# Handing out side work by an engine-time allowance, with loads' copies pinned and sums joined

## The chip, the cores and the metric

The kernel runs on one core of a Trainium2 chip. The metric is device time in microseconds (us) for one execution, from the first to the last instruction and a little around it. Five engines work side by side, each through its own instructions strictly in the order in which they stand: PE (TensorE, matrix products), DVE (VectorE), ACT (ScalarE), POOL (GpSimd) and SP (SyncE, which only issues transfers). An instruction that waits holds up everything behind it on its engine.

## The reference

Four batches of 10048 tokens with 128 channels go through an attention over 49 agents, and the result through a mixture of experts (4 groups of 4 experts, the best group and the best expert of it taken per token).

```python
def sm(a, b):
    s = scale * (a @ b.transpose(0, 2, 1))
    s = s - s.max(-1, keepdims=True)
    e = np.exp(s)
    return e / (e.sum(-1, keepdims=True) + 1e-09)
agent_v = sm(agents, k) @ v          # per batch: 49 x 128
x = sm(q, agents) @ agent_v          # per batch: 10048 x 128
...
g_sm = np.exp(g_logits - g_logits.max(-1, keepdims=True))
g_sm /= g_sm.sum(-1, keepdims=True) + 1e-09      # likewise e_sm in the group
h = np.maximum(xg[mask_e] @ w1[g, e], 0.0)
ye = h @ w2[g, e]
out[tok_idx] = (g_w * e_w)[:, None] * ye
```

## The kernel before

**Units.** The main work is a stream of 644 units. A unit takes one tile of 512 tokens and one eighth of an expert's 1024 hidden columns: `first` (L1139) makes two products into a PSUM tile `ph`, lets ACT write the rectified fp16 part `hh`, and lets DVE write the fp16 remainder `hl` (one `SCALAR_TENSOR_TENSOR` out of `ph` and `hh`); `second` (L1155) makes twelve products into `po` from `hh` and `hl`. There are 3 `ph` tiles, so the products of unit k+3 wait for the `hl` of unit k, and `second` runs 8 units behind `first`. Three batches (positions 0 to 2 in `SEQ`) go through one common expert each, 20 tiles of 8 units, 480 units together; the fourth batch is sorted by expert into DRAM (`sorted_rows`) and makes the last 164 units. Before the first unit, one batch's keys and values are worked off alone.

**Side work.** Everything else is written as Python generators ("lanes") that are drawn on between two units while the program is being written out; a `yield` is a place where the writer may go back to the units, and a `yield n` asks for n units of rest. Lanes `k1` to `k3` (`agents`, L481) do the keys and values of a batch: `xh`, the fp16 part of the keys, on ACT, `xl`, the remainder, on POOL, scores on PE, largest values `mch` on DVE, then `vh` on ACT and `vl` on DVE (`value_split`, L439). Lanes `q0` to `q3` do the queries' weights (`query_exp`, L649: `mq` and `ef` on DVE, the exponential on ACT). Lanes `a0` to `a3` (`followed`, L615) do the routing of five parts of a batch: `routing` (L776) and `weigh` (L817) are long rows of small DVE operations on tiles of 20 columns (`rm`, `rc`, `oh`, `rx`, `rd`, `rrg`, `rre`, `cw`) with two exponentials `rd<-rd` on ACT. `expert_load` and `expert_split` (L1073, L1083) fetch an expert's weights (`w1f`, `w2f`) and split them into fp16 parts. `p3` sends the rows of the sorted batch to DRAM; only when all lanes have ended does `ahead` fetch the first sorted tiles (`er`) and weights (`wbuf<-wdr`).

**What sets the order.** `advance` (L1317) goes through the lanes after each unit. `QUEUE` gives each lane a start and an end in batches; a lane is drawn on for as long as its share of the counted cost `TOTALS` is behind that line, however many steps that takes, and an `a` lane gets up to three steps a unit. `own_tile` and `run_second` draw on a lane by force where a tile needs what isn't there yet. Afterwards a scheduler places each instruction in its engine's order, and may put one ahead of where it was written if it takes its inputs to be there early enough; `keep_in_program_order` pins an instruction behind all that was written for its engine before it.

Of the kernel before, what the change touches and what calls it, by code (L numbers as in the profile page):

```python
# [13 lines left out]
AF = mybir.ActivationFunctionType  # L14
ALU = mybir.AluOpType
# [8 lines left out]
C = 128  # L24
# [4 lines left out]
FB = F // P  # L29
# [21 lines left out]
W2S = 256.0  # L51
# [4 lines left out]
HT = CT // 2  # L56
VS = 16.0
# [8 lines left out]
SORTS = ((0, 5), (5, 10), (10, 15), (15, OT))  # L66
ST = 5 * TQ
ORDER = "kkkkkmkvkvqkqmvvqvvvv"
POOLED = "01001001"
KA = 2  # L70
QUEUE = (("a0", 0.0, 9.0), ("a1", 0.0, 9.0), ("a2", 0.0, 9.0), ("a3", 0.0, 9.0),
# [63 lines left out]
def build(ctx, tc, qT, kT, v, agT, wr, w1, w2, cpk, out):  # L135
    nc = tc.nc
    pool, sync = nc.gpsimd, nc.sync
    work = np.zeros(3)
    pe = Counted(nc.tensor, work, 0, 4.0, 0.42)
    vec = Counted(nc.vector, work, 1, 65.0, 1.04)  # L140
    act = Counted(nc.scalar, work, 2, 190.0, 0.83)
# [127 lines left out]
    clock, forced = [0], [False]  # L269
# [169 lines left out]
    def value_split(b, ci):  # L439

        st = state[b]
        vf = st.pop(("v", ci))
        sh, sl = [mo.tile([P, CT, NA], F16, name=name) for name in ("sh", "sl")]
        vh, vl = [wk.tile([P, CT * P], F16, name=name, tag="x" + name[1]).rearrange("p (t c) -> p t c", c=C) for name in ("vh", "vl")]
        parts = value_parts(b, ci)
        for x, y, m in parts:
            act.activation(vh[0:m, y], vf[0:m, y, 0:C], AF.Copy, scale=VS)
        yield 1
        for x, y, m in parts:
            act.activation(sh[0:m, y], x, AF.Copy)  # L450
            vec.scalar_tensor_tensor(out=vl[0:m, y], in0=vf[0:m, y, 0:C], scalar=VS, in1=vh[0:m, y], op0=ALU.mult, op1=ALU.subtract)
        yield 1
        for x, y, m in parts:
            for a in range(0, x.shape[1], HT):
                z = slice(a, min(x.shape[1], a + HT))
                pool.tensor_sub(out=sl[0:m, y][:, z], in0=x[:, z], in1=sh[0:m, y][:, z])  # L456
        yield
        st["v", ci] = sh, sl, vh, vl
# [190 lines left out]
    def query_exp(b, ci, x, early):  # L649
        t0, t1 = chunks[ci]  # L650
        nt = t1 - t0
        psv = x["ps"][:, 0:nt * NA].rearrange("p (t a) -> p t a", a=NA)
        mq = sm.tile([P, CT], F32, name="mq")
        vec.tensor_reduce(out=mq[:, 0:nt], in_=psv, axis=AX.X, op=ALU.max, negate=True)
        x["ef"] = ef = wk.tile([P, CT, NA], F32, name="ef")
        vec.tensor_add(out=ef[:, 0:nt], in0=psv, in1=mq[:, 0:nt].unsqueeze(2).broadcast_to([P, nt, NA]))
        yield HOP
        act.activation(ef[:, 0:nt], ef[:, 0:nt], AF.Exp)
        yield
# [116 lines left out]
    def routing(b, t0, t1):  # L776

        st = state[b]
        r0 = t0 // ST * ST
        r = t0 // ST  # L780
        lg = st["lg", r]
        if t0 == r0:
            st["ohf", r] = pc.tile([P, NG + NE, ST], F16, name="oh")
            st["g", r] = [pc.tile([P, ST], F32, name=name) for name in ("gm", "zz", "zr")]
        o = st["ohf", r]
        gm, zz, zr = st["g", r]
        flat = lambda a: a.rearrange("p s i t -> p (s i) t")
        t = slice(t0 - r0, t1 - r0)
        pair = lg[:, 0:NG + NE, t].rearrange("p (k j) t -> p k j t", j=2)
        op = o[:, :, t].rearrange("p (k j) t -> p k j t", j=2)  # L790
        mt = sm.tile([P, (NG + NE) // 4, 2, ST], F32, name="rm")[:, :, :, 0:t1 - t0]
        ct = sm.tile([P, (NG + NE) // 4, 2, ST], F16, name="rc")[:, :, :, 0:t1 - t0]
        vec.tensor_tensor(out=op[:, :, 1], in0=pair[:, :, 0], in1=pair[:, :, 1], op=ALU.is_ge)
        vec.tensor_tensor(out=flat(mt), in0=pair[:, :, 0], in1=pair[:, :, 1], op=ALU.max)
        yield
        vec.tensor_tensor(out=ct[:, :, 0], in0=mt[:, :, 0], in1=mt[:, :, 1], op=ALU.is_ge)
        vec.tensor_tensor(out=ct[:, :, 1], in0=mt[:, :, 0], in1=mt[:, :, 1], op=ALU.is_lt)
        vec.tensor_max(out=gm[:, t], in0=mt[:, 0, 0], in1=mt[:, 0, 1])
        vec.tensor_mul(out=op[:, :, 0], in0=op[:, :, 1], in1=flat(ct))
        vec.tensor_sub(out=op[:, :, 1], in0=flat(ct), in1=op[:, :, 0])  # L800
        yield
        og = o[:, 0:NG, t].unsqueeze(2).broadcast_to([P, NG, 4, t1 - t0])
        oh = o[:, NG:, t].rearrange("p (g e) t -> p g e t", g=NG)
        vec.tensor_mul(out=oh, in0=oh, in1=og)
        if t1 == NTP:
            vec.memset(o[:, NG:, NT - r0:], 0.0)
            vec.memset(o[LAST:P, NG:, NT - 1 - r0:NT - r0], 0.0)
        st["oh"] = o[:, NG:, t]
        if t1 % ST == 0:
            sync.dma_start(out=ohd[b][:, r], in_=o[:, NG:])  # L810
        yield
        vec.tensor_scalar(out=zz[:, t], in0=lg[:, NG + NE, t], scalar1=1e-9, scalar2=None, op0=ALU.add)
        vec.reciprocal(out=zr[:, t], in_=zz[:, t])
        vec.tensor_scalar(out=zr[:, t], in0=zr[:, t], scalar1=st["scb"][:, 1:2], scalar2=None, op0=ALU.mult)
        yield

    def weigh(b, t0, t1):  # L817

        st = state[b]
        r = t0 // ST  # L820
        n, t = t1 - t0, slice(t0 - r * ST, t1 - r * ST)
        lg, ohf, g = st["lg", r], st["ohf", r], st["g", r]
        og = ohf[:, 0:NG, t]
        gm, zz, zr = [a[:, t] for a in g]
# [8 lines left out]
        def numerators(x, largest):  # L833
            bc = lambda a: a.unsqueeze(1).broadcast_to([P, 4, n])
            d = sm.tile([P, 4, ST], F32, name="rd")[:, :, 0:n]
            vec.tensor_sub(out=d, in0=x, in1=bc(largest))
            vec.tensor_mul(out=d, in0=d, in1=bc(zr))
            yield HOP
            act.activation(d, d, AF.Exp)
            yield HOP  # L840
            return d

        x = sm.tile([P, NG, 4, ST], F32, name="rx")[:, :, :, 0:n]
# [6 lines left out]
        sg = yield from numerators(lg[:, 0:NG, t], gm)  # L850
        sg = fold(sg, ALU.add, "g")
        yield
        se = yield from numerators(el, fold(el, ALU.max, "m"))
        se = fold(se, ALU.add, "e")
        yield
        for y in (se, sg):
            vec.tensor_scalar(out=y, in0=y, scalar1=1e-9, scalar2=None, op0=ALU.add)
        vec.tensor_mul(out=sg, in0=sg, in1=se)
        vec.tensor_mul(out=sg, in0=sg, in1=zz)
        yield  # L860
        vec.reciprocal(out=sg, in_=sg)
        if t0 == 0:
# [220 lines left out]
    def expert_split(b, x, ws):  # L1083

        w1f, w2f = x["w"]
        for h in range(2):
            ps = bank()
            s = slice(h * 512, (h + 1) * 512)
            pe.matmul(ps, state[b]["at"], w1f[:, s], start=True, stop=True)
            yield HOP  # L1090
            act.activation(ws[:, s], ps, AF.Copy)
            vec.tensor_sub(out=ws[:, F + h * 512:F + (h + 1) * 512], in0=ps, in1=ws[:, s])
            yield
        wv = ws[:, 2 * F:].rearrange("p (k h c) -> p k h c", k=FB, h=2)
        act.activation(wv[:, :, 0], w2f, AF.Copy, scale=W2S)
        yield
        vec.scalar_tensor_tensor(out=wv[:, :, 1], in0=w2f, scalar=W2S, in1=wv[:, :, 0], op0=ALU.mult, op1=ALU.subtract)
        yield

    def kept_expert(b, x, j):  # L1100

# [203 lines left out]
    def step(lane):  # L1305
        if not lane["live"]:
            return 0
        w = work.copy()
        y = next(lane["gen"], "end")
        if y == "end":  # L1310
            lane["live"] = False
        lane["done"] += (y if y in (0, 1) else 0) if lane["name"][0] == "p" else float(np.dot(work - w, WL))
        if lane["name"][0] != "p":
            lane["until"] = clock[0] + (y if isinstance(y, int) else 0)
        return y

    def advance(part):  # L1317
        clock[0] += 1
        for lane in lanes:
            if not lane["live"] or part <= lane["start"]:  # L1320
                continue
            kind = lane["name"][0]
            if kind == "k" and any(y["live"] for y in lanes[:lanes.index(lane)] if y["name"][0] == "k"):
                continue
            if kind == "p":
                if clock[0] % 3:
                    step(lane)
                continue
            if lane["until"] > clock[0]:
                continue  # L1330
            steps = 0
            while lane["live"] and (kind == "a" and steps < 3 or kind != "a" and (part >= lane["end"] or lane["done"] < lane["total"] * (part - lane["start"]) / (lane["end"] - lane["start"]))):
                steps += 1
                if isinstance(step(lane), int):
                    break

    def lane(name):
        return next(y for y in lanes if y["name"] == name)
# [26 lines left out]
    live, fetched, loads = {}, 0, 0  # L1365
# [13 lines left out]
    for pos, i in stream:  # L1379
        if pos < NOWN:  # L1380
            x = own_tile(pos, i)
# [3 lines left out]
        else:  # L1385
# [7 lines left out]
            x = live.pop(i)  # L1393
# [45 lines left out]
```

## Time and profile before

| | us |
|---|---|
| median of 3 runs (1019.42 to 1022.51) | 1021.24 |
| the profiled execution, its own time | 1021.64 |
| its span in the profile | 1019.8 |
| span before the first unit's `hh` | 77.8 |
| units with side work, 78 to 757 us | 679 |
| last own units, almost without side work, 757 to 817 us | 60 |
| sorted units | 187 |

The profile is of one execution. Busy shares over the span are means over these stages: in the last two PE has no idle time, and in the one from 78 to 757 us four engines share the work. The granted clock is PE's, as a share of 2.4 GHz; its other level is 0.5, that is 1.2 GHz.

### The profile page before, as it was taken

The page shows a single profiled execution, that of the slowest core. Times are in us where ns is not written, and L with a number is a line of the kernel's source. Part 1 is how long each engine was busy: PE and PEld are TensorE (multiplying, and loading weights), DVE is VectorE, ACT ScalarE, POOL GpSimd, SP SyncE. Part 2 cuts the span into 40 slices and gives each one's busy share as a digit, 9 for nine tenths or more (in the row PEclk, how much of TensorE's full clock was granted, in tenths as well). Part 3 has the DMA queues.
Part 4 walks back from the last instruction along what each step waited for, and adds up shares of the span by engine and source line. Part 5 has one row for each costly group of instructions (what it writes and reads, how often), then busy time and mean ns, then how long its engine had stood idle before and what let it go on. Part 6 is the DMA issues. An engine that isn't in the chain of part 4 may idle for free.

```text
span 1019.8 us, 31244 instructions
## 1 busy us (share of the span) xinstructions
PE 910.4 (89%) x12947; PEld 725.0 (71%) x12948; DVE 788.2 (77%) x1785; ACT 633.4 (62%) x1086; POOL 430.8 (42%) x569
## 2 busy tenths in 40 slices
PE   3848898899889999899888989899899999999994
PEld 2835677787667778777676777687677877777884
DVE  5636899878879687897897989899786666666663
ACT  4517687676668666867666766665555565555552
POOL 3108643441833354823452244655455114444444
PEclk9778899999999999989999999999999999999998
DMA  9636543332572443724315131213643535544551
GB/s 310 195 107 198 165 126 108 118 96 93 162 223 77 133 125 95 217 85 134 107 46 175 41 113 30 90 57 113 210 166 105 176 129 185 175 162 164 176 192 37
DMA packets 107511, 138.14 MB, mean 135 GB/s; under 512 B 7479, under 2 KB 88186, under 8 KB 104160
## 3 DMA queue, kind: packets, MB, share of 16 engines
q1 hardware_dynamic: 102208, 125.75, 38.9%
q0 software_dynamic: 5152, 10.30, 3.1%
q8 instruction: 103, 1.69, 0.7%
q14 instruction: 48, 0.39, 0.1%
HBM read 96.83 MB, written 39.45 MB: 134 GB/s over the span
## 4 chain that ended last, share of the span: by engine, by line
PE 51%; DVE 23%; issue 7%; ACT 7%; POOL 6%; DMA 5%; SPq 1%; POOLq 0%; ACTq 0%; DVEq 0%
PE po L130 25%; PE ph L130 17%; PE at L130 8%; DVE hl L130 8%; POOL xl L266 4%; DVE vl L130 2%; DMA w2f<-w 2%; ACT hh L130 1%; DMA vf<-v 1%; DVE oh L130 1%; DMA erow<-rows 1%; ACT xh L130 1%; DVE oo L130 1%; DMA out<-oo,er 1%; DVE rrg L130 1%
## 5 line engine op out<-in xcount | busy, mean ns | idle before, releaser
L130 DVE SCALAR_TENSOR_TENSOR hl<-ph,hh 128x512 f16<-128x512 f32 (+1 forms) x644 | 432.4, 680 | 138.9 <-ACT hh L130 137.6
L130 PEld LDWEIGHTS <-hh 128*128 128x128 f16 x5104 | 422.6, 99 | 148.8 <-issue 8.9
L130 PE MATMUL po<-wbuf,hh 128*128 128x128 f16 x5104 | 507.5, 221 | 0.0
L130 ACT ACTIVATE hh<-ph 128x512 f16<-128x512 f32 (+1 forms) x644 | 376.4, 592 | 195.4 <-PE ph L130 194.5
L130 PE MATMUL po<-wbuf,hl 128*128 128x128 f16 x2552 | 468.1, 221 | 0.0
L130 PE MATMUL ph<-et,wbuf 98*128 98x512 f16 (+2 forms) x1312 | 390.3, 380 | 33.4 <-DVE hl L130 31.4
L266 POOL TENSOR_TENSOR xl<-xf,xh 128x256 f16<-128x256 f32 x280 | 188.4, 709 | 200.0 <-ACT xh L130 176.3
L130 PEld LDWEIGHTS <-hl 128*128 128x128 f16 x2552 | 251.5, 99 | 1.5 <-issue 0.3
L130 PEld LDWEIGHTS <-wbuf 98*128 98x128 f16 (+1 forms) x1412 | 108.6, 100 | 59.7 <-issue 41.2
L1192 POOL DMA_INDIRECT out<-oo,er x82 | 80.6, 984 | 137.7 <-ACT hh L130 92.3
L971 POOL DMA_INDIRECT sorted_rows<-rows,slot x79 | 79.7, 1009 | 78.1 <-ACT hh L130 58.7
L456 POOL TENSOR_TENSOR sl<-S,sh 128x245 f16<-128x245 f32 (+2 forms) x51 | 35.3, 716 | 116.2 <-ACT sh L130 104.0
L130 ACT ACTIVATE xh<-xf 128x1280 f16<-128x1280 f32 (+2 forms) x59 | 73.6, 1252 | 16.4 <-PE at L130 10.3
L130 PE MATMUL at<-agh,xl 128*128 128x49 f16 x553 | 56.4, 186 | 9.0 <-POOL xl L266 8.8
L130 PEld LDWEIGHTS <-xh 128*128 128x128 f16 (+1 forms) x1164 | 55.3, 98 | 6.8 <-issue 3.7
L130 PE MATMUL at<-agh,xh 128*128 128x49 f16 x553 | 56.5, 186 | 2.7 <-ACT xh L130 1.3
L130 PEld LDWEIGHTS <-xl 128*128 128x128 f16 x582 | 48.0, 97 | 13.4 <-POOL xl L266 12.9
L130 PE MATMUL at<-agl,xh 128*128 128x49 f16 x553 | 56.0, 185 | 0.0
L130 ACT ACTIVATE et<-at 98x512 f16<-98x512 f16 (+2 forms) x81 | 46.8, 583 | 12.9 <-PE at L130 9.5
L686 POOL TENSOR_TENSOR rows<-ef,rows 128x245 f16<-128x245 f32 (+1 forms) x62 | 38.6, 645 | 36.3 <-ACT rows L130 36.3
L130 DVE SCALAR_TENSOR_TENSOR vl<-vf,vh 128x1280 f16<-128x1280 f32 (+2 forms) x27 | 38.4, 1429 | 5.3 <-ACT vh L130 5.1
L130 DVE TENSOR_TENSOR oo<-po,cw 128x512 f32<-128x512 f32 (+1 forms) x60 | 40.4, 673 | 0.0
(257 smaller groups left out, 948.5 us busy)
## 6 DMA issues: line engine op xcount, KB each, us to landing
wbuf<-wdr SPq DMA_DIRECT2D x22, 1024.0 KB, 4.8
vf<-v SPq DMA_DIRECT2D x28, 640.0 KB, 6.1
xf<-qT SPq DMA_DIRECT2D x28, 640.0 KB, 4.5
xf<-kT SPq DMA_DIRECT2D x23, 640.0 KB, 4.3
out<-oo SPq DMA_DIRECT2D x57, 256.0 KB, 2.7
erow<-rows SPq DMA_DIRECT2D x13, 510.0 KB, 2.8
er<-sorted_rows SPq DMA_DIRECT2D x19, 256.0 KB, 4.8
wbuf<-kT SPq DMA_DIRECT2D x5, 640.0 KB, 6.8
```

Of the source, the lines that this page charges most:

```text
L130: return f(*a, **k)
L266: pool.tensor_sub(out=xl[:, a:z], in0=xf[:, a:z], in1=xh[:, a:z])
L456: pool.tensor_sub(out=sl[0:m, y][:, z], in0=x[:, z], in1=sh[0:m, y][:, z])
L686: pool.tensor_sub(out=x0[:, a:z, NA:2 * NA], in0=ef[:, a:z], in1=x0[:, a:z, 0:NA])
L971: ins = pool.indirect_dma_start(out=sorted_rows[:, :], out_offset=bass.IndirectOffsetOnAxis(ap=at, axis=0), in_=x, in_offset=None, bounds_ ...
L1192: ins = pool.indirect_dma_start(out=out, out_offset=bass.IndirectOffsetOnAxis(ap=to, axis=0), in_=y, in_offset=None, bounds_check=B * N - ...
```

## The change

`advance` now gives all lanes together an allowance per unit, 900 ns of counted DVE time and 1100 ns of counted ACT time (`RATE`). The lane that is furthest behind its line goes first, one step at a time (an `a` lane counts as a whole batch behind, and gets two steps a unit), until either allowance is used up or no lane is behind. An overdraft is taken off the next units; what is left over is not kept. The counted cost is 65 ns and 1.04 ns a column for DVE, 190 ns and 0.83 ns a column for ACT. `QUEUE` and `TOTALS` are unchanged.

Three more edits go with it. The ACT copies that read a fresh load (`vh<-vf` and the `w2f` copy) are pinned in program order. Long pieces are split: `vl` and the remainder of `w2` are made in two halves with a `yield` between, and `query_exp` yields between its two DVE operations. Small sums are joined: the factor on `zr` goes into the exponential's scale, and two additions and two products on `se` and `sg` become two `SCALAR_TENSOR_TENSOR`.

```diff
+RATE = np.array([900.0, 1100.0])
...
         for x, y, m in parts:
-            act.activation(vh[0:m, y], vf[0:m, y, 0:C], AF.Copy, scale=VS)
+            tc.keep_in_program_order(act.activation(vh[0:m, y], vf[0:m, y, 0:C], AF.Copy, scale=VS))
...
-            vec.scalar_tensor_tensor(out=vl[0:m, y], in0=vf[0:m, y, 0:C], scalar=VS, in1=vh[0:m, y], op0=ALU.mult, op1=ALU.subtract)
+        yield
+        for x, y, m in parts:
+            for a in range(0, x.shape[1], HT):
+                z = slice(a, min(x.shape[1], a + HT))
+                vec.scalar_tensor_tensor(out=vl[0:m, y][:, z], in0=vf[0:m, y, 0:C][:, z], scalar=VS, in1=vh[0:m, y][:, z], op0=ALU.mult, op1=ALU.subtract)
+                yield
...
-        vec.tensor_scalar(out=zr[:, t], in0=zr[:, t], scalar1=st["scb"][:, 1:2], scalar2=None, op0=ALU.mult)
...
-            act.activation(d, d, AF.Exp)
+            act.activation(d, d, AF.Exp, scale=st["scb"][:, 1:2])
...
-        for y in (se, sg):
-            vec.tensor_scalar(out=y, in0=y, scalar1=1e-9, scalar2=None, op0=ALU.add)
-        vec.tensor_mul(out=sg, in0=sg, in1=se)
-        vec.tensor_mul(out=sg, in0=sg, in1=zz)
+        vec.scalar_tensor_tensor(out=se, in0=se, scalar=1e-9, in1=zz, op0=ALU.add, op1=ALU.mult)
+        vec.scalar_tensor_tensor(out=sg, in0=sg, scalar=1e-9, in1=se, op0=ALU.add, op1=ALU.mult)
...
-        act.activation(wv[:, :, 0], w2f, AF.Copy, scale=W2S)
+        tc.keep_in_program_order(act.activation(wv[:, :, 0], w2f, AF.Copy, scale=W2S))
...
+    def behind(lane, part):
+        if lane["name"][0] == "a" or part >= lane["end"]:
+            return 1.0
+        span = lane["end"] - lane["start"]
+        return min(1.0, (part - lane["start"]) / span) * span - lane["done"] / lane["total"] * span
+
     def advance(part):
...
-            while lane["live"] and (kind == "a" and steps < 3 or kind != "a" and (part >= lane["end"] or lane["done"] < lane["total"] * (part - lane["start"]) / (lane["end"] - lane["start"]))):
-                steps += 1
-                if isinstance(step(lane), int):
-                    break
+        while min(tokens) > 0:
+            some = [(-behind(y, part), i) for i, y in enumerate(lanes)
+                    if y["live"] and i not in over and part > y["start"] and y["until"] <= clock[0] and behind(y, part) > 0]
+            if not some:
+                break
+            i = min(some)[1]
+            w = work.copy()
+            y = step(lanes[i])
+            steps[i] += 1
+            if isinstance(y, int) or lanes[i]["name"][0] == "a" and steps[i] == 2:
+                over.add(i)
+            tokens[:] -= (work - w)[1:]
```

On ACT, late in the own units, this is how the copies of the last experts' `w2f` (into `ws` and `wbuf`) and of their `w1` products (`ws<-at`) stand before the change, each `hh` row being that many units:

```order
L130 ACTIVATE hh<-ph 128x512 x7
L130 ACTIVATE et<-at 98x512
L130 ACTIVATE hh<-ph 128x512 x7
L130 ACTIVATE ws<-w2f 128x8x128
L130 ACTIVATE hh<-ph 128x512
L130 ACTIVATE et<-at 98x384
L130 ACTIVATE hh<-ph 128x512 x2
L130 ACTIVATE wbuf_119<-w2f 128x8x128
L130 ACTIVATE hh<-ph 128x512
L130 ACTIVATE lg<-at 128x19x21
L130 ACTIVATE hh<-ph 128x512 x2
L130 ACTIVATE wbuf_120<-w2f 128x8x128
```

And the same place with the change:

```order
L131 ACTIVATE rd<-rd,scb_7589 128x80
L131 ACTIVATE hh<-ph 128x512 x13
L131 ACTIVATE ws<-at 128x512
L131 ACTIVATE hh<-ph 128x512 x2
L131 ACTIVATE ws<-at 128x512
L131 ACTIVATE hh<-ph 128x512
L131 ACTIVATE ws<-w2f 128x8x128
L131 ACTIVATE hh<-ph 128x512 x5
L131 ACTIVATE wbuf_119<-at 128x512
```

The first `w2f` copy stood behind the 408th own unit's `hh` and ahead of the products of its own expert; it now stands behind both of them, at the 438th.

On DVE, near the 110th unit, where the first part of the second batch is routed while its successor's keys are worked off, this is what stands between two `hl` before:

```order
L130 SCALAR_TENSOR_TENSOR hl<-ph,hh 128x512
L130 TENSOR_TENSOR oh<-oh,rc 128x10x8
L130 TENSOR_SCALAR zr<-zr,scb_4384 128x8
L130 TENSOR_TENSOR oh<-rc,oh 128x10x8
L130 TENSOR_TENSOR rd<-lg,gm 128x4x8
L130 TENSOR_TENSOR oh<-oh 128x16x8
L130 TENSOR_TENSOR rx<-lg,oh 128x16x8
L130 TENSOR_REDUCE cnt_4815<-oh 128x16
L130 TENSOR_TENSOR rx<-rx 128x8x8
L130 TENSOR_TENSOR rd<-rd,zr 128x4x8
L130 TENSOR_TENSOR rel<-rx 128x4x8
L130 TENSOR_TENSOR rhm<-rel 128x2x8
```

With the change the same routing stands like this:

```order
L131 SCALAR_TENSOR_TENSOR hl<-ph,hh 128x512
L131 TENSOR_TENSOR needf_4727<-at,less 1x16
L131 TENSOR_TENSOR oh<-oh,rc 128x10x8
L131 CAST need_4729<-needf_4727 1x16
L131 TENSOR_TENSOR rd<-lg,gm 128x4x8
L131 TENSOR_TENSOR oh<-rc,oh 128x10x8
L131 TENSOR_TENSOR rd<-rd,zr 128x4x8
L131 TENSOR_TENSOR oh<-oh 128x16x8
L131 TENSOR_TENSOR rx<-lg,oh 128x16x8
L131 TENSOR_REDUCE cnt_4921<-oh 128x16
L131 SCALAR_TENSOR_TENSOR hl<-ph,hh 128x512
L131 TENSOR_TENSOR rx<-rx 128x8x8
```

Before, fourteen small operations follow the `hl` (the last three are cut here); now nine do, and the `zr` product is gone.

## Rows read from the trace of the kernel before

**Rows 1.** The page: busy us (share of the span) and instructions of an engine.

```profile
PE 910.4 (89%) x12947; PEld 725.0 (71%) x12948; DVE 788.2 (77%) x1785; ACT 633.4 (62%) x1086; POOL 430.8 (42%) x569
```

**Rows 2.** The stretch 78 to 757 us: its us, busy us of PE, PEld, DVE, ACT, POOL, granted clock, DMA.

```profile
78.00:757.00 679.00, 617.53 (x9264) 490.92 (x9265) 582.98 (x1393) 464.27 (x802) 315.09 (x446) 0.96 0.40 121
```

**Rows 3.** Waits from 78 to 817 us: total us, times, longest.

```profile
ACT rd L130 <- DVE rd L130: 42.2, 27, 3.4
PE ph L130 <- DVE hl L130: 31.4, 25, 3.9
...
PE at L130 <- POOL xl L266: 8.8, 27, 0.9
...
ACT ws L130 <- DMA w2f<-w: 5.0, 1, 5.0
ACT vh L130 <- DMA vf<-v: 4.5, 2, 2.4
...
ACT wbuf L130 <- DMA w2f<-w: 3.7, 3, 3.3
```

**Rows 4.** ACT's timeline: the first copy of the last experts.

```profile
730.00 1.06 ACT L130 ACTIVATE ws<-w2f 128x1024 f16<-128x1024 f32 x1 [4.98 <-DMA w2f<-w]
```

**Rows 5.** PE's timeline around the first of these waits, and at the other.

```profile
727.05 0.28 PE L130 MATMUL po<-wbuf,hh 128*128 128x128 f16 x2
...
732.96 0.70 PE L130 MATMUL ph<-et,wbuf 98*128 98x512 f16 x2 [3.39 <-DVE hl L130]
733.46 0.42 PE L130 MATMUL po<-wbuf,hh 128*128 128x128 f16 x2
```

**Rows 6.** ACT's and PE's timelines near 545 us, with the second batch's `w2f` copy.

```profile
543.85 1.06 ACT L130 ACTIVATE wbuf<-w2f 128x1024 f16<-128x1024 f32 x1 [3.27 <-DMA w2f<-w]
...
546.82 0.59 PE L130 MATMUL ph<-et,wbuf 98*128 98x512 f16 x2 [2.55 <-DVE hl L130]
```

**Rows 7.** DVE groups, 78 to 817 us: busy us, mean ns, idle before.

```profile
L130 DVE TENSOR_SCALAR zr<-zr,scb 128x20 f32<-128x20 f32 (+2 forms) x18 | 5.9, 327 | 0.0
...
L130 DVE TENSOR_TENSOR rrg<-rrg,rre 128x20 f32<-128x20 f32 (+2 forms) x18 | 5.0, 278 | 0.3
...
L130 DVE TENSOR_TENSOR rrg<-rrg,zz 128x20 f32<-128x20 f32 (+2 forms) x18 | 4.7, 261 | 0.4
...
L130 DVE TENSOR_SCALAR rrg<-rrg 128x20 f32<-128x20 f32 (+2 forms) x18 | 4.4, 244 | 0.0
...
L130 DVE TENSOR_SCALAR rre<-rre 128x20 f32<-128x20 f32 (+2 forms) x18 | 4.1, 226 | 0.2
...
L130 DVE SCALAR_TENSOR_TENSOR avT<-at,za 128x49 f32<-128x49 f32 x3 | 0.6, 207 | 0.1
```

**Rows 8.** Instructions on tiles `vl` and `rrg`: ns min/median/max, first and last start.

```profile
L130 DVE SCALAR_TENSOR_TENSOR vl<-vf,vh x27: 274/1481/2223, 136.2 to 519.6; 128x1280 f16<-128x1280 f32 x21, 128x1024 f16<-128x1024 f32 x3, 64x128 f16<-64x128 f32 x3
...
L130 DVE TENSOR_SCALAR rrg<-rrg x19: 159/168/647, 65.7 to 745.9; 128x20 f32<-128x20 f32 x13, 128x8 f32<-128x8 f32 x3, 128x12 f32<-128x12 f32 x3
```

**Rows 9.** Timelines near 430 us: POOL, DVE and PE.

```profile
423.50 7.25 POOL L266 TENSOR_TENSOR xl<-xf,xh 128x256 f16<-128x256 f32 x12
...
427.01 3.96 DVE L130 TENSOR_TENSOR oh<-lg 128x200 f16<-128x200 f32 x1
...
433.88 1.01 PE L130 MATMUL ph<-et,wbuf 98*128 98x512 f16 x2 [3.94 <-DVE hl L130]
```

**Rows 10.** ACT's timeline just before the first unit.

```profile
72.54 1.06 ACT L130 ACTIVATE wbuf<-w2f 128x1024 f16<-128x1024 f32 x1 [6.19 <-DMA w2f<-w]
...
76.10 1.27 ACT L130 ACTIVATE xh<-xf 128x1280 f16<-128x1280 f32 x1 [2.02 <-DMA xf<-kT]
```

**Rows 11.** Timelines of SP and PE where the sorted units begin.

```profile
797.23 2.97 SPq L1127 DMA_DIRECT2D er<-sorted_rows  x4
801.04 1.19 SPq L1116 DMA_DIRECT2D wbuf<-wdr  x2
...
817.01 1.02 PE L130 MATMUL ph<-et,wbuf 98*128 98x512 f16 x4
```

More of the change, by code (lines that the diff above doesn't have):

```diff
@@ L654, in query_exp @@
         vec.tensor_reduce(out=mq[:, 0:nt], in_=psv, axis=AX.X, op=ALU.max, negate=True)
+        yield
         x["ef"] = ef = wk.tile([P, CT, NA], F32, name="ef")
@@ L1094, in expert_split @@
         wv = ws[:, 2 * F:].rearrange("p (k h c) -> p k h c", k=FB, h=2)
-        act.activation(wv[:, :, 0], w2f, AF.Copy, scale=W2S)
+        tc.keep_in_program_order(act.activation(wv[:, :, 0], w2f, AF.Copy, scale=W2S))
         yield
-        vec.scalar_tensor_tensor(out=wv[:, :, 1], in0=w2f, scalar=W2S, in1=wv[:, :, 0], op0=ALU.mult, op1=ALU.subtract)
-        yield
+        for h in range(2):
+            z = slice(h * FB // 2, (h + 1) * FB // 2)
+            vec.scalar_tensor_tensor(out=wv[:, z, 1], in0=w2f[:, z], scalar=W2S, in1=wv[:, z, 0], op0=ALU.mult, op1=ALU.subtract)
+            yield
     def kept_expert(b, x, j):
@@ L1315, in step @@
         return y
+    tokens = np.zeros(2)
+    def behind(lane, part):
[3 more added lines that the diff above has]
+        return min(1.0, (part - lane["start"]) / span) * span - lane["done"] / lane["total"] * span
     def advance(part):
         clock[0] += 1
[L1319 to L1331, printed above, removed]
-            while lane["live"] and (kind == "a" and steps < 3 or kind != "a" and (part >= lane["end"] or lane["done"] < lane["total"] * (part - lane["start"]) / (lane["end"] - lane["start"]))):
-                steps += 1
-                if isinstance(step(lane), int):
-                    break
+        np.minimum(tokens + RATE, RATE, out=tokens)
+        over = set()
+        steps = dict.fromkeys(range(len(lanes)), 0)
+        for i, y in enumerate(lanes):
+            if y["name"][0] == "k" and any(z["live"] for z in lanes[:i] if z["name"][0] == "k"):
+                over.add(i)
+            if y["name"][0] == "p":
+                over.add(i)
+                if y["live"] and part > y["start"] and clock[0] % 3:
+                    step(y)
+        while min(tokens) > 0:
[8 more added lines that the diff above has]
+            if isinstance(y, int) or lanes[i]["name"][0] == "a" and steps[i] == 2:
+                over.add(i)
+            tokens[:] -= (work - w)[1:]
     def lane(name):
```

## The prediction

> **What bounds the kernel now.** I read the page first for the shares, then the stretches, then the waits, and only then the timeline at the longest ones. PE is busy for 89% of the span and DVE for 77% [rows 1]. These means hide that the change touches one stretch only: 78 to 757 us, the 430 or so units with side work between them. There PE is idle for 679 - 617.5 = 61.5 us while DVE works for 583.0 of 679 us (86%), ACT for 464.3 (68%) and POOL for 315.1 (46%) [rows 2]. The reader should see that no engine is full, and that the two that are closest to it take turns in being late. The granted clock is 0.96 there [rows 2]; with levels of 1.0 and 0.5, the shortage of 0.04 is 54 us at the lower level, and 27 us of work at full clock that did not get done.
>
> The waits say who PE waits for: `ph` for an `hl` of DVE in 31.4 us, 25 times, up to 3.9 us, and scores for POOL's `xl` in 8.8 us [rows 3]. A `ph` that waits for `hl` is a queue gone dry: three `ph` tiles let PE run about three units ahead, so DVE, or ACT in front of it, must have been late by that much. The timelines at three of the longest show two kinds of lateness. At 730 us ACT stands 4.98 us before a copy of `w2f` that hasn't landed [rows 4], every `hh` behind it waits too, and PE loses 3.39 us [rows 5]; at 543.85 the same with 3.27 us on ACT and 2.55 us on PE [rows 6]. At 427 us it is DVE alone: one `oh<-lg` of 200 columns takes 3.96 us while POOL works through twelve pieces of `xl`, more small operations stand behind it ahead of the next `hl`, and PE loses 3.94 us [rows 9]. After a loss of this size PE also runs slow for a while: a pair of `po` products takes 0.42 us behind the stall of 733 us against 0.28 us ahead of it [rows 5].
>
> **The change part by part.**
>
> *Pinned copies.* With the change the `w2f` copy stands behind its expert's two `w1` products, and for the last experts it moves by thirty units, from 408 to 438. The transfer has landed by then. That takes away PE's 3.39 and 2.55 us [rows 5, 6]. The `vh` copies waited 4.5 us in two places [rows 3], of which I count 1 us on PE, since a wait of 2.4 us or less is about what three `ph` tiles cover. A: -7 us. Bounds: 0, if the wait moves with the copy, and -10.4 us, if all of the `vh` wait counts.
>
> At the start the same pin costs something. The copy of the first batch's `w2f`, at 72.54 us, lies in time in which ACT would wait for a key load anyway, until 76.10 [rows 10]. Pinned, it comes after that load's copy and ahead of the first `hh`: D: +1 us, the copy's own 1.06 us; 0 if the earlier `w1` copy gives the time back.
>
> *Joined sums.* For each of 18 parts of a batch in this stretch DVE loses `zr` times the factor (327 ns), two additions (244 and 226) and two products (278 and 261) [rows 7], 1336 ns. It gains two `SCALAR_TENSOR_TENSOR` of the same size, which the trace doesn't have. The nearest rows are one of 49 columns at 207 ns, and the product of the same operands at 278 [rows 7]. I take 260, since the shape and the operands are the product's: 1336 - 520 = 816 ns, times 18 is 14.7 us of DVE (14.0 to 16.6 by the two rows). The factor now goes into the exponential on ACT, which has a third of its time free.
>
> *Halves.* Splitting `vl` gives 24 more instructions and the `w2` remainders 5. What an extra start costs is read from the smallest and the middle `vl`: 274 ns for 128 columns and 1481 for 1280 [rows 8], so 1.05 ns a column and 140 ns for the start. 29 x 0.14 = 4.1 us. Below, it costs nothing where DVE would have waited. Net, DVE loses 10.6 us of 583. Not all of it reaches the end: DVE is the late one only at the waits. These sums do stand in just the crowded places, so I count somewhat under half. B: -4 us, from 0 to -12.5.
>
> *The allowance.* The longest row of small operations between two `hl` near unit 110 goes from fourteen to nine, about a third off; the key chunks of the second batch, which came in units 110 to 123, now come in 114 to 135. The lateness that can be had back this way is what DVE and POOL still cost PE after A: 31.4 - 5.9 + 8.8 = 34 us [rows 3, 5, 6]. I take a quarter. A third would match the shorter row, but POOL's pace is untouched and the allowance is loose: it counts 65 ns and 1.04 ns a column, 86 ns for an operation of 20 columns that takes 226 to 327 ns [rows 7]. Ten of them fit into a unit, some 2.5 us. C: -8 us. With fewer long stalls less time at the lower clock follows: a quarter of the 27 us above is 7, and half of that is on time that PE sets, so -3 us. Bounds of both: 0, and -34 - 14 = -48.
>
> *What lies behind.* The side work ends later: the expert splits run to unit 455, past 435, and `p3` ends behind unit 467 instead of 460, so the first fetch of sorted tiles and weights comes some 7 units of 1.1 us later, 8 us. It started at 797.23 and its weights were issued at 801.04, for products at 817.01 [rows 11]. 16 us of cover become 8 us, and the cover is gone if the weights need more than that. I count 0, at most +3 us.
>
> Sum against the profiled execution's own time of 1021.64, which is 0.4 us over the median: 1021.6 - 7 + 1 - 4 - 8 - 3 = 1000.6, so **1001 us**.
>
> **A rule weighed against the rows.** One `oh<-lg` took 3.96 us with POOL at work beside it [rows 9], and an addition on 20 columns that takes 159 ns at best and 168 in the middle took 647 [rows 8]. The Trainium skill, GPSIMD Engine Reference, section Specifications, says that GpSimd's SBUF interfaces are shared with VectorE, with contention for VectorE instructions that have two SBUF inputs or a two-port mode. The trace agrees at 427 us, with 3.96 us. By that rule joining sums helps less than the count, since the joined ones have two SBUF inputs as well, and small operations that are spread over more units meet POOL more often.
>
> **The rivals.**
>
> *Only the loads and the sums.* The allowance is too loose to matter, since its prices are a third of the measured ones, and the bursts stay. For it: the price per operation above. Against it: the row of nine where fourteen stood. A and D whole and half of B: 1021.6 - 7 + 1 - 2 = about 1013.5 us.
>
> *POOL takes it back.* There are some 25 small operations in each of 18 parts, 450 in all. A collision costs up to 0.65 - 0.17 = 0.48 us [rows 8], and POOL is at work for 46% of the time [rows 2]. The mean `rrg` addition of 244 ns against 168 [rows 7, 8] says that now one in six collides. If it became one in three, DVE would get 450 x 0.16 x 0.48 = 35 us more; a third of that on the path is 12 us. The sum is then 1021.6 - 7 + 1 - 4 - 11 + 12 = 1012.6 us with C whole and 1023.6 without it. Since collisions make just the bursts that C is to shorten, I put this case at 1018 to 1023 us. The rule above is about this one.
>
> *The exponentials hold ACT.* ACT stood 42.2 us, 27 times, before `rd<-rd` for DVE's product [rows 3], with the next `hh` behind it. The new order still leaves about one unit between the product and its exponential, and spreading a chain over more units puts more `hl` ahead of the product. If each of the 36 exponentials waited the longest of 3.4 us [rows 3], the sum would be 122 us, 80 more. A wait beyond 2.4 us comes through to PE by about 1 us each, 36 us; half of them would do: 1021.6 - 7 + 1 - 4 + 18 = about 1029.6 us, slower. It decides from about 12 more such waits on. Against it: the allowance takes work from ahead of these products as well.
>
> **How the numbers follow.** The forecast has a chance of 0.58, loads and sums only 0.20, POOL 0.12, the exponentials 0.10. The range is 988 to 1020 us: below it lies the forecast with half of C's bound (0.05), above it the exponentials and half of the POOL case (0.16 together). The forecast's own range is 988 to 1012. About 0.3% is what a measurement of this kernel can tell from no change, 1018.2 to 1024.3 us. Forecast and first rival give 0.58 + 0.17 faster and 0.03 the same; POOL 0.02, 0.08 and 0.02; the exponentials 0.01 the same and 0.09 slower: faster 0.77, same 0.12, slower 0.11.
>
> **What would show it.** A: no wait of ACT on a `w2f` transfer past 78 us. B: no `zr<-zr,scb`, the joined ones near 260 ns, DVE's busy time in the stretch 572 us or so. C: `ph` waiting for `hl` for 20 us or less, no single wait over 3 us, and a granted clock of 0.97 or more. D: the first `hh` at about 79 us. It is wrong if `ACT rd` waits 60 us or more, if small operations get slower on average, or if PE stands idle ahead of the first sorted unit.

## The result, and the profile after

The changed kernel takes 1005.59 us (median of four executions, 1003.51 to 1008.70) against 1021.11 us for the kernel before: a ratio of 0.9851, with a 95% interval of 0.9821 to 0.9881. It is faster by 15.5 us; 1001 us was forecast, with a range of 988 to 1020. Ratios, here and below, are taken over the executions within 1.5% of the fastest of the same kernel. The execution shown took 1003.51 us. Its page, with each engine's busy time, answers to [rows 1]:

```profile
PE 900.1 (90%) x12947; PEld 718.8 (72%) x12948; DVE 784.7 (78%) x1758; ACT 636.3 (64%) x1086; POOL 426.2 (43%) x569
```

The same stretch as in [rows 2], in the same columns:

```profile
78.00:757.00 679.00, 624.51 (x9491) 498.17 (x9492) 590.94 (x1388) 475.38 (x818) 315.90 (x450) 0.98 0.40 122
```

In these 679 us PE now gets through 9491 matmuls instead of 9264. It is idle for 54.5 us instead of 61.5, and the granted clock is 0.98 instead of 0.96. DVE is busier than before here since more units fall into the stretch; over the whole page it has lost 3.5 us, where 10.6 were forecast. Over the whole page PE is idle for 101.7 us of its span of 1001.8 (109.4 of 1019.8 before) and is busy for 10.3 us less than in [rows 1], for the same 12947 matmuls: in these two profiles more than half of the gain is in faster matmuls (the ends of matmuls are modelled in a profile).

The waits from 78 to 817 us answer to [rows 3]:

```profile
ACT rd L131 <- DVE rd L131: 33.6, 28, 2.7
...
PE ph L131 <- DVE hl L131: 25.1, 28, 2.1
...
PE at L131 <- POOL xl L267: 8.3, 22, 0.9
...
ACT xh L131 <- DMA xf<-kT: 5.1, 3, 3.6
...
PE at L131 <- ACT xh L131: 3.4, 1, 3.4
```

No row says that ACT waits for `w2f` or `vf`: those 13 us are gone. PE waits 6.3 us less for `hl`, and the longest such wait is 2.1 us where it was 3.9. The last two rows show a wait that has grown: ACT waited 1.6 us for a key load before, once, and PE had no such wait behind it. The timeline of SP, ACT and PE shows where it comes from:

```profile
271.32 0.35 SPq L1082 DMA_DIRECT2D w1f<-w  x1
271.87 0.41 SPq L1083 DMA_DIRECT2D w2f<-w  x1
272.46 1.52 SPq L237 DMA_DIRECT2D xf<-kT  x2
...
279.24 1.27 ACT L131 ACTIVATE xh<-xf 128x1280 f16<-128x1280 f32 x1 [3.63 <-DMA xf<-kT]
...
280.57 0.22 PE L131 MATMUL at<-agh,xh 128*128 128x49 f16 x1 [3.44 <-ACT xh L131]
```

SP issues the next expert's weight loads and then, behind them, the key load that ACT needs first. That load took 6.7 us to land, against 4.3 in the median of this kernel's key loads of that size. So 3.4 us of what was gained elsewhere are given back here; no run changes the order of the loads, so that the weight loads are the cause is likely, not shown.

DVE's groups of the joined sums and of the remainders, as in [rows 7]: busy us, mean ns, idle before.

```profile
L131 DVE SCALAR_TENSOR_TENSOR vl<-vf,vh 128x640 f16<-128x640 f32 (+2 forms) x51 | 43.0, 849 | 5.5 <-ACT vh L131 5.5
...
L131 DVE TENSOR_TENSOR S<-S,mb 128x490 f32<-128x490 f32 (+2 forms) x27 | 19.8, 751 | 0.1
...
L131 DVE SCALAR_TENSOR_TENSOR rre<-rre,zz 128x20 f32<-128x20 f32 (+2 forms) x18 | 4.8, 268 | 0.4
...
L131 DVE SCALAR_TENSOR_TENSOR rrg<-rrg,rre 128x20 f32<-128x20 f32 (+2 forms) x18 | 4.8, 268 | 0.2
```

The joined sums take 268 ns where 260 was assumed.

### The profile page after: what moved, and what is told of

Read it like the earlier page. It is cut to its first block, busy times and chain, and to the rows that moved or that the text cites. A ratio compares the mean times of both kernels' runs of the same rounds, so it can differ in the third digit from the quotient of the medians.

```text
span 1001.8 us, 31196 instructions
## 1 busy us (share of the span) xinstructions
PE 900.1 (90%) x12947; PEld 718.8 (72%) x12948; DVE 784.7 (78%) x1758; ACT 636.3 (64%) x1086; POOL 426.2 (43%) x569
## 4 chain that ended last, share of the span: by engine, by line
PE 51%; DVE 27%; DMA 6%; POOL 5%; ACT 5%; issue 5%; SPq 1%; POOLq 0%; DVEq 0%; ACTq 0%
PE po L131 25%; PE ph L131 17%; DVE hl L131 10%; PE at L131 8%; POOL xl L267 4%; DVE vl L131 2%; DMA xf<-kT 2%; ACT hh L131 2%; DVE oh L131 1%; DVE oo L131 1%; DMA erow<-rows 1%; DVE rd L131 1%; DVE mq L131 1%; DVE ef L131 1%; DVE rx L131 1%
## 5 line engine op out<-in xcount | busy, mean ns | idle before, releaser
L131 PE MATMUL po<-wbuf,hh 128*128 128x128 f16 x5104 | 501.7, 220 | 0.0
L131 PE MATMUL ph<-et,wbuf 98*128 98x512 f16 (+2 forms) x1312 | 386.3, 377 | 26.9 <-DVE hl L131 25.1
L267 POOL TENSOR_TENSOR xl<-xf,xh 128x256 f16<-128x256 f32 x280 | 183.8, 691 | 211.1 <-ACT xh L131 168.1
L131 ACT ACTIVATE xh<-xf 128x1280 f16<-128x1280 f32 (+2 forms) x59 | 73.6, 1253 | 20.5 <-PE at L131 10.6
L693 POOL TENSOR_TENSOR rows<-ef,rows 128x245 f16<-128x245 f32 (+1 forms) x62 | 40.7, 678 | 70.5 <-ACT rows L131 69.2
L131 PEld LDWEIGHTS <-xl 128*128 128x128 f16 (+1 forms) x582 | 48.9, 98 | 12.3 <-POOL xl L267 12.0
L131 DVE SCALAR_TENSOR_TENSOR vl<-vf,vh 128x640 f16<-128x640 f32 (+2 forms) x51 | 43.0, 849 | 5.5 <-ACT vh L131 5.5
```

The source lines that it names most:

```text
L131: return f(*a, **k)
L267: pool.tensor_sub(out=xl[:, a:z], in0=xf[:, a:z], in1=xh[:, a:z])
L693: pool.tensor_sub(out=x0[:, a:z, NA:2 * NA], in0=ef[:, a:z], in1=x0[:, a:z, 0:NA])
```

## The experiments

The first theory was the prediction's own: the pins give 7 us, the allowance about 11 with what the clock follows, the sums 4. The rival was the first of the prediction: the allowance is too loose to do anything. Kernels were timed in three groups, on three chips, each against the kernel before on that chip (medians 1028.0, 1027.6 and 1019.4 us), so ratios are compared rather than times. The kernel before has one profile, which was taken ahead of these groups.

A ratio says nothing of the way in which time was saved. Every timed execution also lists its span and its mean granted clock, so I split the gain in two. (1 - clock) x span is the time that the lowered clock would cost if PE set the pace throughout; for the kernel before in the first group it is 0.0432 x 1026.1 = 44.3 us. What is left of the span is the second part. Both are averaged over the executions of a kernel and subtracted from those of before. The mean clock differs by 0.0035 from one execution to the next, so each part is uncertain by some 3 to 4 us. It is a rough estimate, since the clock's mean also runs over time in which PE does not set the pace. Ahead of the first unit this is plain to see. The stretch from 20 to 60 us, first in the profile above and then in that of the same kernel's last run below:

```profile
20.00:60.00 40.00, 30.73 (x323) 27.27 (x323) 20.48 (x46) 15.37 (x26) 8.27 (x10) 1.00 0.59 177
```

```profile
20.00:60.00 40.00, 30.29 (x323) 26.86 (x323) 20.63 (x47) 15.23 (x25) 8.27 (x10) 0.83 0.59 178
```

The second profile spends a third of it at the lower level, which the split counts as 6.8 us; yet both get through the same 323 matmuls, and their first `hh` comes at 78.0 and 78.2 us. Over the 150 executions behind the table, each set against the mean of its kernel on its chip, a mean clock higher by 0.010 goes with a span that is 3.1 us shorter (least squares), where the split would say 10. So the clock's column is no measured size of what the clock gave.

| kernel | ratio (95%) | clock, this / before | gain by the clock, us | other gain, us |
|---|---|---|---|---|
| allowance alone | 1.0024 (1.0003-1.0045) | 0.9592 / 0.9568 | 2.4 | -4.7 |
| both pins alone | 0.9851 (0.9824-0.9878) | 0.9653 / 0.9568 | 9.3 | 6.2 |
| changed, old planner | 0.983 (0.9784-0.9877) | 0.9625 / 0.9568 | 6.5 | 10.8 |
| changed, no pins | 0.9944 (0.9919-0.9968) | 0.9665 / 0.9568 | 10.2 | -4.6 |
| `w2f` pin alone | 0.9939 (0.9915-0.9964) | 0.9616 / 0.9590 | 2.9 | 4.2 |
| `vh` pin alone | 0.992 (0.9893-0.9947) | 0.9656 / 0.9590 | 7.0 | 1.4 |
| changed, key copies pinned too | 0.9938 (0.9916-0.9959) | 0.9681 / 0.9590 | 9.5 | -3.3 |
| changed, no cap | 0.985 (0.9802-0.9898) | 0.9625 / 0.9590 | 4.1 | 11.9 |
| sums alone | 0.9956 (0.9932-0.9979) | 0.9624 / 0.9612 | 1.4 | 3.4 |
| both pins and sums | 0.9867 (0.9826-0.9907) | 0.9647 / 0.9612 | 4.1 | 10.4 |
| changed, true prices | 1.0162 (1.0132-1.0192) | 0.9504 / 0.9612 | -11.7 | -3.9 |
| the changed kernel again | 0.9865 (0.9835-0.9895) | 0.9664 / 0.9612 | 5.8 | 8.5 |

**The allowance alone.** The kernel before with `RATE`, `tokens`, `behind` and the new loop in `advance`, nothing else.

> The kernel before with the allowance alone: no pins, no halves, no joined sums. Theory (the allowance shortens DVE's bursts, the pins take two waits for w2f, and both pay again through a higher granted clock): the w2f waits on ACT stay (5 us and 3 us), PE's wait for hl falls to about 25 us, and the time is 1011 us, ratio 0.990 (0.986 to 0.994). Rival, pins alone make the gain: 1021 us, ratio 1.000. Rival, the small sums make it: 1021 us too.

Measured: 1.0024, no gain and rather a loss. Its waits from 78 to 817 us are those of before:

```profile
PE ph L131 <- DVE hl L131: 29.1, 29, 3.7
...
ACT wbuf L131 <- DMA w2f<-w: 7.7, 4, 2.4
ACT ws L131 <- DMA w2f<-w: 3.2, 1, 3.2
ACT vh L131 <- DMA vf<-v: 2.7, 1, 2.7
```

The theory falls: PE waits for `hl` about as long as in [rows 3], and so does ACT for its loads, 13.6 us against 13.2.

**The pins alone.** The kernel before with two lines changed:

```
-            act.activation(vh[0:m, y], vf[0:m, y, 0:C], AF.Copy, scale=VS)
+            tc.keep_in_program_order(act.activation(vh[0:m, y], vf[0:m, y, 0:C], AF.Copy, scale=VS))
-        act.activation(wv[:, :, 0], w2f, AF.Copy, scale=W2S)
+        tc.keep_in_program_order(act.activation(wv[:, :, 0], w2f, AF.Copy, scale=W2S))
```

> The kernel before with the two pinned copies alone. Theory: the two waits for w2f at 545 and 730 us are gone, 6 us of PE and up to 2 us of low clock, 1013 us, ratio 0.992. Rival, pins alone make the gain: 1006 us, ratio 0.985. Rival, the wait moves with the copy: ratio 1.000.

Measured: 0.9851, the ratio of the whole change, as the rival said. Its page, its stretch of 78 to 757 us and its wait of PE for `hl`:

```profile
PE 902.7 (89%) x12947; PEld 720.3 (71%) x12948; DVE 784.6 (78%) x1785; ACT 629.5 (62%) x1086; POOL 428.3 (42%) x569
```

```profile
78.00:757.00 679.00, 625.83 (x9439) 497.39 (x9440) 592.07 (x1414) 472.16 (x818) 320.15 (x452) 0.97 0.41 125
```

```profile
PE ph L130 <- DVE hl L130: 20.9, 24, 2.9
```

PE is idle for 53.2 us, 8.3 less than before, and waits 10.5 us less for `hl`, with the old planner and the old sums. Over the page PE is busy for 7.7 us less than in [rows 1], for the same matmuls; against the allowance alone, which gained nothing on the same chip, it is 10.8 us less busy and 7.5 less idle. The split has 6.2 us beside the clock, as forecast for this step, and 9.3 by the clock. So about half of this gain is in faster matmuls, which the forecast gave to the allowance and at 3 us.

**All but the allowance.** The changed kernel with the loop of `advance` of before.

> All edits but the allowance: pins, halves and joined sums on the old way through the lanes. Theory: A and B without C, 1010 us, ratio 0.989; more than 20 us at the lower clock stay from 100 us on. Rival, the allowance gives nothing: 1006 us, ratio 0.985. Rival, finer steps without an allowance only give the old planner more to bunch: ratio 0.995 or above.

Measured: 0.983, no slower than the changed kernel. Its six executions spread from 1002.6 to 1021.1 us, though, and the ratio of the medians of all six would be 0.9877. By itself this run doesn't settle whether the allowance gives the last 2 or 3 us.

**All but the pins.** The changed kernel with both copies as before.

> The changed kernel without the two pins. Theory: one or two waits of ACT for w2f of 3 to 5 us come back, with PE idle by 5 to 6 us behind them and a stretch at the lower clock: 1013 us, ratio 0.992. Rival, under the allowance the copies are late enough anyway: 1006 us, ratio 0.985. Rival, pins alone make the gain: 1020 us, ratio 0.999.

Measured: 0.9944. Of the change's 15 us about 6 remain, and the waits for loads are back. PE's and ACT's waits from 78 to 817 us:

```profile
PE ph L131 <- DVE hl L131: 33.7, 41, 4.1
...
ACT wbuf L131 <- DMA w2f<-w: 9.0, 4, 3.6
...
ACT vh L131 <- DMA vf<-v: 5.1, 1, 5.1
ACT ws L131 <- DMA w2f<-w: 4.1, 1, 4.1
```

With the pins alone this settles where the gain is: 15 us when the pins come by themselves, some 10 when they come on top of the other edits. The clock's mean does not tell these kernels apart: without the pins it is 0.9665, the highest of the group. Next, which of the pins makes the gain, and why more than the 7 us of the visible loss.

**The `w2f` pin alone.** The second of the two lines above.

> The kernel before with the w2f copies pinned and the vh copies not. New theory, after the pins alone gave the whole gain (ratio 0.985) and the allowance alone nothing: time in which ACT stands for a load comes through almost whole, whoever PE waits for by name, since DVE starves behind ACT and has no free time to make it up. Of 14.8 us of such waits before, 8.7 are for w2f: ratio 0.9915 (0.989 to 0.994). Rival, only what PE visibly loses counts: 6 us, ratio 0.994. Rival, the two pins act together through the buffers that vf and w2f share: each alone gives less than a third, ratio 0.996 or above.

Measured: 0.9939, 6.3 us: what PE visibly lost in [rows 5, 6]. The theory's 0.9915 and the second rival's 0.996 lie at the two edges of the interval.

**The `vh` pin alone.** The first of the two lines.

> The kernel before with the vh copies pinned and the w2f copies not. New theory, waits for loads on ACT come through whole: 4.5 us of the 14.8 are for vf, ratio 0.9956 (0.993 to 0.998). Rival, only what PE visibly loses counts: 1 us, ratio 0.999. Rival, the pinned vh also thins out the order of the value chunks, and that is the larger part of the gain: ratio 0.991 or below.

Measured: 0.992, 8.2 us, though ACT had waited only 4.5 us for `vf` in the kernel before [rows 3]. That only PE's visible loss counts is excluded; between the other two the interval does not decide. The page and the stretch:

```profile
PE 902.9 (89%) x12947; PEld 718.7 (71%) x12948; DVE 784.9 (77%) x1785; ACT 629.0 (62%) x1086; POOL 425.3 (42%) x569
```

```profile
78.00:757.00 679.00, 618.65 (x9360) 491.10 (x9358) 586.32 (x1406) 467.48 (x811) 312.88 (x447) 0.98 0.40 123
```

PE is idle for 60.4 us, 1.1 less than before, just the 1 us that the prediction counted. But the clock is 0.98 instead of 0.96, and PE is busy for 7.5 us less than in [rows 1] for the same matmuls. In the timed executions the clock is 0.9656 instead of 0.9590, which the split counts as 7.0 us. Together the two pins give 0.61 + 0.80 = 1.41%, against 1.49% for both in one kernel: they add up. Whether it is the vanished wait for `vf` or the new place of the copies that keeps the clock up isn't told apart by this: a third buffer for `vf` with the copies left free might do so; it was not tried.

**The key copies pinned as well.** In the changed kernel, for the wait at 279 us:

```
-        act.activation(xh[:, 0:n], xf[:, 0:n], AF.Copy)
+        tc.keep_in_program_order(act.activation(xh[:, 0:n], xf[:, 0:n], AF.Copy))
```

> The changed kernel with the xh copies of keys and queries pinned as well. The changed kernel still has 5.1 us of ACT waiting for key loads, 3.6 of it at 279 us with 3.4 us of PE behind it. New theory: that wait goes or shrinks below 1.5 us, ratio 0.981 (0.978 to 0.984) against 0.985 for the changed kernel. Rival, a copy placed later only moves the wait to POOL's xl and PE's scores: ratio 0.985 or above.

Measured: 0.9938, against 0.985 without the cap on the same chip (below): more than half of the gain lost, as the rival said. The wait itself stays:

```profile
PE ph L131 <- DVE hl L131: 28.1, 33, 2.1
PE at L131 <- POOL xl L267: 9.7, 24, 2.3
ACT xh L131 <- DMA xf<-kT: 4.4, 1, 4.4
PE at L131 <- ACT xh L131: 4.4, 1, 4.4
```

A pin helps where the scheduler had put a copy ahead of its load. Here the load itself comes late, again right behind SP's two weight loads, and the pin can't bring it forward. That the rest is lost because the other 58 copies of this line can no longer be placed freely is an argument; no run shows it.

**No cap.** The changed kernel with `RATE = np.array([9000.0, 11000.0])`, ten times the allowance.

> The changed kernel with an allowance ten times as large, so that it never binds; the rule that the lane furthest behind goes first stays, and two steps for an a lane. Theory that the allowance is too loose to matter: ratio 0.985, the same as the changed kernel within 0.003. Rival, the allowance does bind and helps: ratio 0.990 or above. Rival, it binds and hurts: 0.981 or below.

Measured: 0.985. Without any effective limit the kernel is as fast: the allowance as it stands decides nothing that is measured.

**The sums alone.** The kernel before with the joined sums and the scale in the exponential.

> The kernel before with the joined sums alone: the two additions and two products of a router group become two joined instructions, and the scale moves into the exponentials. Every wait on a load and the old planner stay. The prediction's step: the sums take about 0.8 us of VectorE time from each of 18 router parts, 14.7 us in all, and give about 4 us (ratio 0.996), spread thinly over the sorted image's own stage. The rival after the runs so far: the joined edits without the pins gave about 0.6 per cent at most together with the allowance, and on top of the pins nothing, so the sums alone stay within 0.3 per cent of 1, because in this stage VectorE's saved time only moves which of its instructions meets GpSimd. A ratio of 0.993 to 0.997 holds for the step, 0.998 to 1.002 for the rival.

Measured: 0.9956, 4.5 us. By themselves the sums give what the prediction said, and the rival's range of 0.998 to 1.002 is missed. In its stretch DVE is busy for 574.2 us, 8.8 less than before, with some more units in it:

```profile
78.00:757.00 679.00, 619.19 (x9315) 491.49 (x9314) 574.17 (x1348) 468.35 (x806) 314.09 (x444) 0.97 0.40 122
```

**Both pins and the sums.** Without halves and allowance.

> The kernel before with the two pinned copies and the joined sums, without the halved remainders and without the allowance. If the sums give their 4 us beside the pins: ratio about 0.981, better than the pins alone at 0.985 and than the changed kernel. If the pins make the whole gain, as the runs so far say: 0.984 to 0.987, the same as the changed kernel itself in this call. In both cases the waits of ScalarE for value and expert loads are under 1 us in all.

Measured: 0.9867, the same as the changed kernel beside it (0.9865). Its stretch has the least idle time of PE of the kernels that were not slower, 49.3 us:

```profile
78.00:757.00 679.00, 629.73 (x9448) 501.10 (x9449) 584.22 (x1362) 475.67 (x818) 319.99 (x452) 0.97 0.41 125
```

Beside the clock it gains 10.4 us, near to the 6.2 + 3.4 of its two parts. The whole gain doesn't add up, though: 1.49% and 0.44% would be 0.981, which lies outside the interval of 0.9826 to 0.9907. On top of the pins the sums give nothing that is measured, the second of the two cases. The pins, with or without the sums, thus give what the whole diff gives, and no version here is clearly faster.

**True prices.** The changed kernel, with the allowance fed by what the trace shows a VectorE instruction to cost:

```
-            self.work[self.i] += self.fixed + each * float(np.prod(x.shape[1:]))
+            n = each * float(np.prod(x.shape[1:]))
+            self.work[self.i] += self.fixed + n
+            if self.i:
+                self.work[self.i + 2] += (170.0 if self.i == 1 else self.fixed) + n
```

and `RATE` 1000 and 1100; the two new counters feed the allowance alone.

> The changed kernel with the allowance's prices set by the trace: each VectorE instruction counts 170 ns of fixed time rather than 65, against 1000 ns of VectorE and 1100 ns of ScalarE a unit, so that the allowance binds; the order written for the engines moves by up to some 40 units for the second sample's value chunks. If the allowance failed only because its prices made it too loose, side work now really stands evenly, the first product's waits for the remainder of the hidden layer (25 us in the changed kernel) fall to about 15 us and the kernel is 5 to 8 us faster than the changed one (ratio about 0.978). If bursts of side work were never what these waits come from (each unit's own chain is short of time anyway), it is as the changed kernel, 0.983 to 0.987; if work pushed later crowds the end of the stage, it is slower than that, 0.988 to 0.995.

Measured: 1.0162, slower than before, so the third case, and far outside its range. But the trace shows two things at once. From the first unit to the 479th `hh` it takes 708 us. The changed kernel again, on the same chip, takes 721 us. First this kernel, then that, each over its own stretch:

```profile
78.00:786.00 708.00, 660.79 (x9963) 527.26 (x9962) 597.36 (x1422) 492.68 (x848) 303.78 (x442) 0.98 0.38 116
```

```profile
78.00:799.00 721.00, 666.46 (x9972) 530.28 (x9972) 619.44 (x1434) 497.68 (x857) 331.73 (x466) 0.97 0.41 124
```

For the same matmuls PE is idle for 47.2 instead of 54.5 us. Behind that stretch it takes 41 us more than the changed kernel, so the 13 us are lost three times over. The indirect transfers that write `sorted_rows`, in this kernel and then in the changed one (ns min/median/max, first and last start):

```profile
L978 POOL DMA_INDIRECT sorted_rows<-rows,slot x79: 976/983/1472, 685.4 to 817.4; - x79
```

```profile
L975 POOL DMA_INDIRECT sorted_rows<-rows,slot x79: 969/978/1290, 639.1 to 787.5; - x79
```

They start 46 us and end 30 us later, and the first fetch of a sorted tile waits for the last of them. PE's timeline there:

```profile
822.45 0.66 PE L134 MATMUL at<-ident,er 128*98 128x128 f16 x4 [25.42 <-DMA er<-sorted_rows]
```

PE also runs slow behind that wait:

```profile
822.40:837.00 14.60, 8.60 (x39) 4.62 (x40) 2.97 (x5) 5.38 (x9) 0.00 (x0) 0.51 0.93 361
```

So with an allowance that binds the stage is shorter, and the work that it puts off lands on the one chain that ends the stage. Some of the 13 us is only lent, since POOL has 28 us and DVE 22 us less to do in this kernel's stretch than in the other; how much, no run tells, and an allowance between the two was not tried.

**The changed kernel again,** on the chip of the last three.

> The changed kernel itself, on the same chip as the three above, so that they can be read against it: 0.985, as in its first runs, with 25 us of waits of the first product for the remainder of the hidden layer. All theories expect the same; a ratio off by more than 0.4 per cent would say that the size of the whole gain depends on the chip.

Measured: 0.9865, and PE waits 25.6 us for `hl`, as in the profile above (25.1).

## Why the prediction came out right, and which terms did not

The sum of 1001 us missed 1005.6 by 4.6 us and the direction held. That the sum came so near is luck: the pins alone gave 15 us where 7 were counted, the allowance nothing where 11 were, and the sums nothing measured beside the pins where 4 were, and these errors cancel. By its mechanism the first rival, which had a chance of 0.20, comes nearer to what was found than the forecast with 0.58.

**A, the pinned copies: mis-sized.** The mechanism is right: no wait for `w2f` past 78 us, and PE has 8.3 us less idle time with the pins alone, 7.0 in the changed kernel, for the 7 forecast. But the pins alone give 15 us. The `w2f` pin gives the 6 that were counted for it; the `vh` pin was counted with 1 and gives 8.2. The term left out the clock: "-7 us" counted stalls, and the lower level that follows stalls stood under the allowance. With the pins alone PE is busy for 7.7 us less for the same matmuls, with the `vh` pin alone 7.5 us. The bound of -10.4 us was too near for the same reason. How the `vh` pin does it stays open.

**B, the sums: right alone, not beside the pins.** The five instructions of a part took 1336 ns [rows 7] and are two of 268 now, so 800 ns x 18 = 14.4 us against 14.7. Alone they give 4.5 us for the 4 forecast, and on top of the pins nothing that is measured (0.9867 against the 0.9851 of the pins alone). The halves cost DVE what was said (`vl` 43.0 us in 51 instead of 38.4 in 27 with the pins and the sums) and bring nothing that is measured. In the whole kernel `S<-S,mb` also takes 751 ns in the mean; with the sums alone it took 627:

```profile
L130 DVE TENSOR_TENSOR S<-S,mb 128x490 f32<-128x490 f32 (+2 forms) x27 | 16.2, 627 | 0.1
```

That eats 3.6 us of DVE's saving. In all but one of the kernels with halves it takes 672 to 751 ns, in those without 610 to 652; true prices, with halves, has 633. Why was not tested.

**C, the allowance: wrong.** "A quarter" of 34 us and 3 us of clock were forecast; alone it gives a ratio of 1.0024, and with ten times the allowance the changed kernel is no slower. The step that failed is the reading of the order: nine small operations where fourteen stood at one place were taken for a binding limit. The reason against it was in the text, 86 ns counted for an operation that takes 226 to 327. The first rival said just this of the allowance, but its sum of 1013.5 us had the pins too low. In the profile after, PE's wait for `hl` of 25.1 us is above the 20 that C asked for. C's other two signs came true without it: the longest wait is 2.1 us and the clock 0.98, but the pins alone show 2.9 and 0.97 as well. They could not tell C from A.

**D, the start: about as said.** The first `hh` comes at 78.0 us, 77.8 before, so this pair doesn't show the copy's 1.06 us. But over all profiles it comes at 75.3 to 77.8 us in the five kernels without the `w2f` pin, 76.4 in the mean, and at 76.1 to 79.5 us in the nine profiles with it, 77.9 in the mean.

**What lies behind: right here.** The first sorted weights are issued at 791.97 us for products at 798.99: 16 us of cover became 7, for the 8 forecast, and no gap of PE stands ahead of the first sorted unit. With true prices this cover is what fails, by 25.4 us.

**The other rivals.** ACT waits 33.6 us for `rd`, not 60 or more, so the exponentials do not hold it. POOL does not take the gain back. Its sign, that small operations get slower, did come, but small: the 594 on DVE between 78 and 817 us that average under 500 ns and stand in both traces in the same number take 164.7 us instead of 159.8, where the rival counted 35 more.

## What to carry to other kernels

Before anything is evened out, look for copies that wait for a load on an engine that works in order: two one-line pins gave the gain of the whole diff, while a pin on copies whose load itself comes late made things worse. Count a stall twice, once as idle time and once as the lower clock behind it, and check the second by PE's busy time for the same matmuls. A sign that several causes would give tells none of them apart. A limit in a planner has to be priced from the trace: this one, at a third of the measured price, did nothing. When it does bind, look first whether the chain that ends the stage is among the work that it puts off.

## What the runs showed of the hardware

In the profiles, faster matmuls are as large a part of a gain of 15 us as idle time: for the same 12947 matmuls PE is busy for 910.4 us in the kernel before, 900.1 in the changed kernel, 902.7 with the pins alone and 902.9 with the `vh` pin alone, the last with 1.1 us less idle time from 78 to 757 us. The share is not fixed: with both pins and the sums it is 905.7, and more of the gain is idle time. Each is one profile, and the changed kernel's last run has 901.7. The mean granted clock is a poor measure of it. It varied by 0.0035 (standard deviation) from one execution of a program to the next: the changed kernel shows 0.974 in the profile above and 0.960 to 0.968 in its other three executions. Part of that lay in a stretch where it cost nothing, 0.83 against 1.00 from 20 to 60 us with the first `hh` at 78.2 and 78.0 us. A wait of 25.4 us left PE at a clock of 0.51 for the next 14.6 us.
